# Backward pass of a convolution block with a gated product: one slab's pass over dh becomes a pass over two slabs with 512 columns

## The chip, the cores and the metric

The kernel runs on one core of a Trainium2 chip, in one launch. The metric is the device time in microseconds (us), the median of several runs. The engines of the core are named as the profile names them: PE multiplies matrices (PEld is its weight load, which runs beside it), DVE and ACT work on vectors, POOL and SP here mostly issue transfers. A transfer that is issued by SP, ACT or POOL stands in that engine's own queue, and an engine works its instructions off in order.

## The reference, cut to what matters

There are 2048 rows (S), 1024 columns (D) and 3584 hidden columns (F). The reference returns the output and the gradients of this function with respect to q, k, v, the taps, the filters and the three weight matrices:

```python
def _A_ref(q, k, v, shift_k, ssm_k, ssm_D):      # per column: 4 taps, then a long convolution
    k_shift = sum(k_pad[:, t:t + S, :] * shift_k[:, 3 - t] for t in range(4))
    kv = k_shift * v
    y = causal_conv(kv, ssm_k) + kv * ssm_D      # by FFT of length 2 S
    return q * y
def _B_ref(x, w_gate, w_up, w_down):
    g, u = x @ w_gate, x @ w_up
    h = g * u
    return h @ w_down
xn = _layernorm(A_q)
out = A_q + _A_ref(xn, k, v, ...) * silu(_B_ref(xn, w_gate, w_up, w_down))
```

The change concerns mostly the gradient of `_B_ref`. With dB the gradient of its result, dh = dB @ w_down.T, then dg = dh * u and du = dh * g, and the weight gradients are xn.T @ dg, xn.T @ du and h.T @ dB.

## The kernel before, in words

The work stands in one program whose parts overlap. In the order of PE's time:

1. Layer norm, and the gate and up products, in 14 slabs of 256 hidden columns (`gu_unit`, L655). u and g of a slab go to the buffer GUd in memory. The forward convolution runs on DVE beside it in `conv_forward` (L740); `shift` (L758) multiplies k by the taps, which lie spread over all partitions in `Wbc` (L128), four taps by 1024 columns. `spread` (L150) fills `Wbc` from memory, through POOL's queue.
2. The down product and the gate (`late_mm`, L1368, and `gate`, L1296). It leaves dB in memory (DBMd) and, turned, in four buffers DBMT (U10, U8, U4, U5), one for each 512 rows.
3. The stage of dh and of the two weight gradients, L1447 to L1552. It is the one that is changed most, and is described below.
4. The gradient of w_down (L1587), and then the gradient of the input with the layer norm's backward pass (`dx_part`, L1641, `ln_backward`, L1664). Beside that DVE works off the gradient of k and of the taps (`dk_units`, L1204), which reads `Wbc` again.

In stage 3 a half (`dh_half`, L1471) is dh of one slab for 1024 rows. It has two groups g of four row blocks. A matmul takes a 128 x 128 block of DBMT as its weights and the slab's turned rows of w_down, `wdt`, as the moving operand with 256 columns (L1482). Eight of them add up one row block, and two row blocks share one PSUM tile of 512 columns. ACT copies each tile into `dht` (L1484). When a group is complete, `multiply` (L1487) multiplies u and g of these four blocks by dht on DVE, in place (one instruction of 128 x 2048, recorded under the helper's line L212); after the second group the whole tile is stored to DGd through SP. u and g of a half come in through SP beforehand (`gu_in`, L1343): one of five buffers of 1 MB, two or three halves ahead.

`dw_slab` (L1495) has eight steps dc, one for each 128 columns of D. A step is 16 matmuls of 512 columns over all 2048 rows (L1499), with the first half's tile for rows 0 to 1023 and the second half's for the rest. ACT copies the sum into `wb` (three buffers, each for two steps), and SP stores it. After each step one group of the next slab's dh runs (`next(others)`), so that dh of slab s + 1 is spread over steps 0 to 3 of slab s. `load_wdt` (L1328) turns the 256 rows of w_down for slab s + 2 on the way in, through SP, in step 3 of slab s (two buffers, in the pool `bw`).

Beside it DVE works off the backward convolution: first eight forward transforms of dy (`dy_forward`, L1080), whose results go to memory (DYFd) through POOL, then 16 products and inverse transforms. `btick` (L1459) hands DVE so much of this work after each group on PE as keeps both in step. From the start of stage 3 DVE's instructions are kept in the order in which the program writes them; the same holds for POOL's transfers. ps_b has four PSUM tiles, in turn, for the groups of L1482 and L1499.

Of the kernel before, what the change touches and what calls it, by code (L numbers as in the profile page):

```python
# [19 lines left out]
def build_kernel(  # L20
# [107 lines left out]
    Wbc = const.tile([P, 4, D], BF16, name="Wbc")  # L128

    tip = tc.alloc_tile_pool(name="tip", bufs=1)  # L130
    TI = tip.tile([P, 2, 8, 2, P], BF16, name="TI")
# [9 lines left out]
    def load_bcast(bsb):  # L141

        wrow = bsb.tile([1, D, 4], BF16, name="wrow")
        st(wrow[:].rearrange("p d j -> p (d j)"), A_shift_k.rearrange("(o d) j -> o (d j)", o=1))
        wtap = bsb.tile([1, 4, D], BF16, name="wtap")

        def turn(j):
            nc.gpsimd.tensor_copy(wtap[:, j, :], wrow[:, :, j])

        def spread():  # L150
            st(WTd.rearrange("(o x) -> o x", o=1), wtap[:].rearrange("p j d -> p (j d)"))
            st(Wbc[:].rearrange("p j d -> p (j d)"), bass.AP(WTd.tensor, WTd.offset, [[0, P], [1, 4 * D]]))
        return turn, spread

    def angles(tg):
# [378 lines left out]
    Dz = kst.tile([P, D], BF16, name="Dz")  # L534
    V.memset(Dz[:], 0.0)
    krow = kst.tile([P, 2, 11, 256], BF16, name="k")
    V.memset(krow[0:1, 0, 0:3, :], 0.0)
    bsb = pool("bc_sb", 1)
    tg = pool("tg", 1)
# [200 lines left out]
    def conv_forward():  # L740
        S_ = conv_state

        def load_kv(dp, c):
            S_["k", dp] = krow
            if dp > 0 or c == 0:
                for i in range(2) if dp == 0 else (c,):
                    cld_k(krow[:, i], i, dp)
            if dp > 0 or c == 1:
                for i in range(2) if dp == 0 else (c,):
                    v = U[4][:, 2048 * i:2048 * i + 2048].rearrange("p (a x) -> p a x", a=8)  # L750
                    cld_v(v, i, dp * 256, 256)
# [6 lines left out]
        def shift(dp):  # L758
            kv = cx.tile([P, NB, 256], BF16, name="kv")
            S_["kvt", dp] = kv  # L760
            k = S_.pop(("k", dp))
            wb = lambda j: Wbc[:, j:j + 1, dp * 256:(dp + 1) * 256].unsqueeze(1).to_broadcast([P, 2, 8, 256])
# [12 lines left out]
            yield 2.3  # L775
# [294 lines left out]
    while conv_state["filters"]:  # L1070
        bm_first([fc_])
        fc_ += 1
    bw = pool("bw", 2, side="right")
    mh = [pool("mh0", 1, side="right")]
    ps_bx = pool("ps_bx", 1, space=PSUM)

# [106 lines left out]

    def dh_tail(ds, G, ew):
        hr = ew.tile([P, 2, 8, P], BF16, name="yl")
        ho = ew.tile([P, 2, P, 8], BF16, name="ho")
        for c in range(2):
            for rq in range(2):
                ps = ps_y4[0].tile([P, 4, P], F32, name="psY")
                for i in range(4):  # L1190
                    r = 4 * rq + i
                    for k in range(2):
                        nc.tensor.matmul(ps[:, i, :], G[:, 2 * r + k, c * P:(c + 1) * P], TI[:, 0, r, k, :],  # L1193
                                         start=(k == 0), stop=(k == 1))
# [9 lines left out]
    def dk_units(ew):  # L1204
# [9 lines left out]
        def load_turned(i):  # L1214
# [7 lines left out]
                nc.sync.dma_start_transpose(out=dkT[:], in_=DKSHd[ds, c * H:c * H + H, :])  # L1222
            return kT, dkT

        dk = load_rows(0)
        yield 3
        for i in range(16):
            ds, c = divmod(i, 2)
            dsl = slice(ds * P, (ds + 1) * P)
            wb = lambda j: Wbc[:, j:j + 1, dsl].to_broadcast([P, 8, P])  # L1230
# [95 lines left out]
            defer(turn)  # L1326

    def load_wdt(sl):  # L1328
        wdt = bw.tile([P, DC, SLW], BF16, name="wdt")
        wdt_ld[0] = nc.sync.dma_start_transpose(out=wdt[:], in_=B_w_down[sl * SLW:(sl + 1) * SLW, :])  # L1330
        return wdt

    def load_ht(bp):
        ht = mh[bp % 2].tile([P, NF, 256], BF16, name="ht")
# [1 line left out]
            last = ld(ht[:, f0:f1], ht_rows(bp, f0, f1))  # L1336
        return (lambda fc: ht[:, fc]), last

    DGU = {}
    wdts = []  # L1340
    wdt_ld = [None]

    def gu_in(k):  # L1343

        if k < 2 * NSL:
            t = U[(11, 6, 2, 3, 12)[k % 5]][:].rearrange("p (a b f) -> p a b f", b=8, a=2)
            ld(t, GUd[k // 2, k % 2])
            DGU[k] = t

    with tc.issue_after(ht1[1].ins):  # L1350
        ht2 = load_ht(2)
    bm_first(range(fc_, NF))
    room = [bw.tile([P, DC, SLW], BF16, name="wdt")[:].rearrange("p (i x) f -> p i (x f)", i=2) for i in range(2)]
# [61 lines left out]
    for bp in range(2, 8):  # L1415
# [6 lines left out]
        with tc.issue_after(row_ld[0].ins):  # L1422
            if bp in (4, 5, 7):
                q = (4, 5, 7).index(bp)
                dma_t = nc.sync.dma_start_transpose(out=DBMT[q], in_=DBMd[512 * q:512 * q + 512, :])
            if bp == 6:
                wdts.append(load_wdt(0))
                dma_t = wdt_ld[0]
        with tc.issue_after(dma_t.ins) if dma_t is not None else nullcontext():
            rows_in[2 * bp + 1] = gate_rows(2 * bp + 1)  # L1430
        if bp > 5:
            with tc.issue_after(row_ld[0].ins):
                gu_in(0) if bp == 6 else wdts.append(load_wdt(1))
        for i in range(2):
            n = (2 * bp + i - 2) * NF
            while done < n + NF:
# [11 lines left out]

    XN = [u8(q, a=4) for q in (7, 0, 1, 9)]
    bg = pool("bg", 2, side="right")  # L1450
    U.append(bg.tile([P, 4096], BF16, name="U12", bufs=1))
    ps_b = ps_tr = pool("ps_b", 4, space=PSUM)
    tr_name[0] = "psb"
    ps_c3 = pool("ps_c3", 2, space=PSUM)
# [6 lines left out]
        bpump((bcnt[0] - 10) / (BT - 10))  # L1461

    todo = []

    def after_group(n):
        flush(2)
# [1 line left out]
            todo.pop(0)()  # L1468
        btick(n)

    def dh_half(k, wdt):  # L1471

        sl, hf = divmod(k, 2)
        dgu = DGU[k]
        for g in range(2):
            dht = bg.tile([P, 4, SLW], BF16, name="dht", bufs=3)
            for e in range(2):
                ps = ps_b.tile([P, 512], F32, name="psb")
                for x in range(2):
                    b = 4 * g + 2 * e + x  # L1480
                    for dc in range(DC):
                        nc.tensor.matmul(ps[:, x * SLW:(x + 1) * SLW], DBMT[2 * hf + g][:, dc, (b % 4) * P:(b % 4 + 1) * P],  # L1482
                                         wdt[:, dc, :], start=(dc == 0), stop=(dc == DC - 1))
                nc.scalar.copy(out=dht[:, 2 * e:2 * e + 2].rearrange("p b f -> p (b f)"), in_=ps[:])  # L1484
                after_group(1)

            def multiply(g=g, dht=dht):  # L1487
                bs = slice(4 * g, 4 * g + 4)
                tt(dgu[:, :, bs], dgu[:, :, bs], dht[:].unsqueeze(1).to_broadcast([P, 2, 4, SLW]), MUL)
                if g == 1:  # L1490
                    ld(DGd[sl, :, 1024 * hf:1024 * hf + 1024, :].rearrange("a (u b) f -> u a b f", u=P), dgu)
            todo.append(multiply)
            yield

    def dw_slab(sl, dgus, others):  # L1495
        for dc in range(DC):
# [28 lines left out]
    for k in (3, 4):  # L1525
        gu_in(k)
    DBM = [u8(q, a=4) for q in (10, 8, 4, 5)]
    HSL = (3, 11, 6)
    hs = {}
    PIN[0] = PINQ[0] = True  # L1530
    for k in range(2):
        run(dh_half(k, wdts[0]))
    todo.pop()()
    for sl in range(NSL):
        if sl + 1 == NSL:
            load_h(0)
            for q in range(4):
                ld(DBM[q], DBMd[512 * q:512 * q + 512, :].rearrange("(b u) d -> u b d", u=P))
            load_h(1)

        def halves():
            for k in (2 * sl + 2, 2 * sl + 3):
                if k < 2 * NSL:
                    yield from dh_half(k, wdts[sl + 1])
        dw_slab(sl, [DGU[2 * sl], DGU[2 * sl + 1]], halves())
        for k in (2 * sl + 5, 2 * sl + 6):
            gu_in(k)
# [260 lines left out]
```

## Time and profile before

| what | before |
|---|---|
| median of 3 runs (lowest to highest) | 1911.96 us (1911.43 to 1912.38) |
| the profiled execution's own time | 1911.63 us |
| its span, first to last instruction | 1909.9 us |
| PE busy | 1899.4 us (99%), 11379 matmuls |
| PEld, DVE, ACT, POOL busy | 1013.9, 1549.7, 636.8, 332.7 us |
| PE busy from 0 to 700 us, 700 to 1317 us | 693.01 of 700, 616.88 of 617 us |
| PE busy from 1317 to 1506 us, 1506 to 1910 us | 189.00 of 189, 400.46 of 404 us |
| DVE busy in the same four stretches | 628.03, 546.51, 151.45, 223.70 us |
| granted clock of PE in all of them | 1.00 |
| share of the DMA engines in them | 0.79, 0.77, 0.83, 0.82 |
| chain that ended last | 97% PE |

Stage 3 runs from 700 to 1317 us. Matmuls are pipelined in the records: the "mean ns of one" of a group is how long one is on its way, and the pace is read from a run of them (a row of the chain or of the timeline says how many started in which time). A row of the timeline gives the start in us, the time in us, the engine, the line, the operation, output and inputs, the count, and in brackets the idle time before it and what ended it. SPq and POOLq are the instructions that issue transfers.

### The profile page before, as it was taken

The page shows a single profiled execution, that of the slowest core. Times are in us where ns is not written, and L with a number is a line of the kernel's source. Part 1 is how long each engine was busy: PE and PEld are TensorE (multiplying, and loading weights), DVE is VectorE, ACT ScalarE, POOL GpSimd, SP SyncE. Part 2 cuts the span into 40 slices and gives each one's busy share as a digit, 9 for nine tenths or more (in the row PEclk, how much of TensorE's full clock was granted, in tenths as well). Part 3 has the DMA queues.
Part 4 walks back from the last instruction along what each step waited for, and adds up shares of the span by engine and source line. Part 5 has one row for each costly group of instructions (what it writes and reads, how often), then busy time and mean ns, then how long its engine had stood idle before and what let it go on. Part 6 is the DMA issues. An engine that isn't in the chain of part 4 may idle for free.

```text
span 1909.9 us, 28150 instructions
## 1 busy us (share of the span) xinstructions
PE 1899.4 (99%) x11379; PEld 1013.9 (53%) x11379; DVE 1549.7 (81%) x1711; ACT 636.8 (33%) x927; POOL 332.7 (17%) x465
## 2 busy tenths in 40 slices
PE   8999999999999999999999999999999999999999
PEld 5555555545444466666666665664444444444444
DVE  8999999999988556887999999999995305788862
ACT  5765555556333233432222222222222102111121
POOL 5121211201113220001031221211212101111120
PEclk9999999999999999999999999999999999999999
DMA  9777766769769997677897798585887999989852
GB/s 298 269 263 233 251 208 223 252 211 311 241 227 307 316 314 231 209 231 233 264 277 247 231 266 258 184 286 180 230 238 181 219 206 190 194 187 190 194 166 88
DMA packets 425106, 444.34 MB, mean 233 GB/s; under 512 B 268400, under 2 KB 342796, under 8 KB 410512
## 3 DMA queue, kind: packets, MB, share of 16 engines
q1 hardware_dynamic: 367504, 239.03, 45.9%
q0 software_dynamic: 41152, 174.15, 29.0%
q10 hardware_dynamic: 16320, 29.36, 4.1%
q8 instruction: 89, 1.46, 0.3%
q14 instruction: 41, 0.34, 0.1%
HBM read 193.87 MB, written 189.84 MB: 201 GB/s over the span
## 4 chain that ended last, share of the span: by engine, by line
PE 97%; DVE 1%; ACT 1%; DMA 0%; issue 0%; SPq 0%; ACTq 0%
PE psb L1499 20%; PE psx L1644 20%; PE psg L671 19%; PE psb L1482 10%; PE psbm L1034 10%; PE psb L1582 9%; PE psF L234 3%; PE psI L455 1%; PE tr L565 1%; PE psY L1193 1%; PE psY L445 1%; PE psx L1582 1%; DVE bst L578 0%; DMA wslab<-in_B_w_gate_dram 0%; PE tr L788 0%; DVE U L212 0%
## 5 line engine op out<-in xcount | busy, mean ns | idle before, releaser
L671 PE MATMUL psg<-wslab,U 128*128 128x512 bf16 x1792 | 401.8, 379 | 3.5 <-DMA wslab<-in_B_w_gate_dram 2.1
L1499 PE MATMUL psb<-U,U 128*128 128x512 bf16 x1792 | 397.1, 379 | 0.0
L1644 PE MATMUL psx<-U,dgut 128*128 128x512 bf16 x1536 | 332.8, 379 | 0.0
L1644 PEld LDWEIGHTS <-dgut 128*128 128x128 bf16 x1792 | 175.3, 98 | 211.4
L1499 PEld LDWEIGHTS <-U 128*128 128x128 bf16 x1792 | 175.2, 98 | 198.0
L671 PEld LDWEIGHTS <-U 128*128 128x128 bf16 x1792 | 172.6, 98 | 197.2 <-issue 3.6
L1482 PE MATMUL psb<-wdt,U 128*128 128x256 bf16 x1792 | 205.6, 273 | 0.0
L1482 PEld LDWEIGHTS <-U 128*128 128x128 bf16 x1792 | 175.2, 98 | 29.2
L212 DVE TENSOR_TENSOR W<-W 128x1024 f32<-128x1024 f32 (+1 forms) x189 | 186.5, 1003 | 4.1
L1582 PE MATMUL psb<-U,U 128*128 128x512 bf16 x816 | 177.3, 379 | 0.0
L1504 ACT CAST wb<-psb 128x512 bf16<-128x512 f32 x112 | 65.6, 586 | 315.4 <-PE psb L1499 310.5
L1249 DVE SCALAR_TENSOR_TENSOR dkp<-dkT,kT 128x1024 bf16<-128x1024 bf16 (+2 forms) x64 | 78.3, 1223 | 93.1 <-DMA dkT<-DKSHd 91.4
L1034 PE MATMUL psbm<-U,ht 128*128 128x512 bf16 x672 | 146.0, 379 | 0.0
L1582 PEld LDWEIGHTS <-U 128*128 128x128 bf16 x896 | 87.4, 98 | 104.4
L673 ACT CAST gut<-psg 128x512 bf16<-128x512 f32 x156 | 91.5, 589 | 120.2 <-PE psg L671 119.7
L1676 ACT ACTIVATE dx_t<-dxn 128x1024 bf16<-128x1024 f32 x15 | 15.9, 1057 | 324.7 <-DVE dxn L212 324.7
L1034 PEld LDWEIGHTS <-ht 128*128 128x128 bf16 x672 | 65.7, 98 | 78.1
L212 DVE TENSOR_TENSOR U<-U,dht 128x2048 bf16<-128x2048 bf16 x56 | 68.3, 1220 | 46.5 <-ACT dht L1484 46.5
L1484 ACT CAST dht<-psb 128x512 bf16<-128x512 f32 x112 | 65.6, 587 | 116.4 <-PE psb L1482 116.4
L66 POOL DMA_DIRECT2D Hd<-hN x54 | 36.6, 677 | 268.9 <-DVE hN L212 258.9
L1623 ACT CAST wbs<-psb 128x512 bf16<-128x512 f32 x51 | 29.9, 586 | 145.4 <-PE psb L1582 134.3
L212 DVE TENSOR_TENSOR W<-SP 128x1024 f32<-128x1024 f32 x64 | 74.1, 1218 | 1.3 <-ACT SP L295 0.8
(263 smaller groups left out, 2342.9 us busy)
## 6 DMA issues: line engine op xcount, KB each, us to landing
U<-GUd SPq DMA_DIRECT2D x28, 1024.0 KB, 9.3
DGd<-U SPq DMA_DIRECT2D x28, 1024.0 KB, 5.8
GUd<-gut ACTq DMA_DIRECT2D x39, 512.0 KB, 5.2
out_dram<-wb SPq DMA_DIRECT2D x112, 128.0 KB, 4.8
U<-Hd SPq DMA_DIRECT2D x14, 1024.0 KB, 6.6
Hd<-hN POOLq DMA_DIRECT2D x54, 256.0 KB, 4.5
HTd<-hT SPq DMA_DIRECT2D x24, 512.0 KB, 3.7
ht<-HTd SPq DMA_DIRECT2D x18, 512.0 KB, 7.5
```

The costliest lines, as they stand in the source:

```text
L212: pinned(V.tensor_tensor(o, a, b, op))
L234: mm = nc.tensor.matmul(ps[:, k].rearrange("p (c d) -> p c d", c=2), T[:, r, k, :], xr[:, r], start=(n == 0), stop=(n == len(rs) - 1 and ( ...
L671: gu_mm[0] = nc.tensor.matmul(ps[:], XNT[q][:, dc, qi * P:(qi + 1) * P], w[:, dc].rearrange("p a f -> p (a f)"), start=(dc == 0), stop=(dc ...
L673: nc.scalar.copy(out=gut[:, :, i], in_=ps[:].rearrange("p (a f) -> p a f", a=2))
L1034: mm = nc.tensor.matmul(ps[:, dh * 512:(dh + 1) * 512], ht(fc)[:, i * P:(i + 1) * P], WD[fc // 4][:, fc % 4, dh * 512:(dh + 1) * 512], sta ...
L1249: ins = V.scalar_tensor_tensor(prod[:].rearrange("p r d -> p (r d)")[:, lo:H], dkT[:, 0, lo:H], 1.0, kT[:, 0, 13 + m + lo:13 + m + H], op0 ...
L1482: nc.tensor.matmul(ps[:, x * SLW:(x + 1) * SLW], DBMT[2 * hf + g][:, dc, (b % 4) * P:(b % 4 + 1) * P], wdt[:, dc, :], start=(dc == 0), sto ...
L1484: nc.scalar.copy(out=dht[:, 2 * e:2 * e + 2].rearrange("p b f -> p (b f)"), in_=ps[:])
L1499: nc.tensor.matmul(ps[:], XN[b // 4][:, b % 4, dc * P:(dc + 1) * P], dgus[b // 8][:, :, b % 8], start=(b == 0), stop=(b == NB - 1))
L1504: nc.scalar.copy(out=wb[:, dc % 2].rearrange("p a f -> p (a f)"), in_=ps[:])
L1582: nc.tensor.matmul(ps, h[:, f, b, :], DBM[b // 4][:, b % 4, dh * 512:(dh + 1) * 512], start=(b == 0), stop=(b == NB - 1))
L1644: nc.tensor.matmul(ps[:, dh * 512:(dh + 1) * 512], t[n][:, f, i * P:(i + 1) * P], WGU[n][:, f, dh * 512:(dh + 1) * 512], start=(n == 0 and ...
```

## The change

dh is now worked out for two slabs at a time. A matmul takes the same weights, and as its moving operand 2 x 256 columns, those of both slabs; eight of them fill a PSUM tile for one row block. Halves and groups are kept: `dh_pair(p, hf)` is dh of slabs 2p and 2p + 1 for 1024 rows. Half 0 of pair p + 1 runs in steps 4 to 7 of slab 2p, half 1 in steps 2 to 5 of slab 2p + 1 (two PSUM tiles behind each of these steps); pair 0 runs ahead of slab 0. `multiply` does one instruction for each slab of the pair, so two in a row. `dht` of the first group has one buffer of its own, that of the second uses half of the table TI, which nothing reads any more.

The turned rows lie in four buffers (WDT): two in `bw` and two in a new tile of `bg`. They are loaded a pair ahead, four before the stage and the others in step 5 of odd slabs and step 1 of even ones. u and g have six buffers instead of five (U13 is added) and are loaded in another order.

The room comes from the taps. `Wbc` (1024 columns for the whole kernel) is gone. `WB` holds two quarters of 256 columns; the first two are loaded in one transfer on SP's queue, the third and fourth on POOL's just ahead of the loads of k. `dk_units` loads its own quarters (`wbk`, two buffers), through POOL. `ho` of the last inverse transforms shares a buffer with `vl`.

```diff
-            st(Wbc[:].rearrange("p j d -> p (j d)"), bass.AP(WTd.tensor, WTd.offset, [[0, P], [1, 4 * D]]))
+            load_taps(WB[:].rearrange("p j e d -> p j (e d)"), 0, 512, ld)
...
+            if dp > 1 and c == 0:
+                load_taps(WB[:, :, dp % 2], dp * 256, 256)
...
+            if i % 4 == 0:
+                wbk = ew.tile([P, 4, 256], BF16, name="wbk", bufs=2)
+                load_taps(wbk[:], ds * P, 256)
...
-    def dh_half(k, wdt):
+    def dh_pair(p, hf):
+        if 2 * p >= NSL:
+            return
+        both = (2 * p, 2 * p + 1)
         for g in range(2):
-            dht = bg.tile([P, 4, SLW], BF16, name="dht", bufs=3)
-            for e in range(2):
+            dht = bg.tile([P, 4, 2, SLW], BF16, name="dht", bufs=1)[:] if g == 0 else dht_own
+            for x in range(4):
                 ps = ps_b.tile([P, 512], F32, name="psb")
-                for x in range(2):
-                    b = 4 * g + 2 * e + x
-                    for dc in range(DC):
-                        nc.tensor.matmul(ps[:, x * SLW:(x + 1) * SLW], DBMT[2 * hf + g][:, dc, (b % 4) * P:(b % 4 + 1) * P],
-                                         wdt[:, dc, :], start=(dc == 0), stop=(dc == DC - 1))
-                nc.scalar.copy(out=dht[:, 2 * e:2 * e + 2].rearrange("p b f -> p (b f)"), in_=ps[:])
+                for dc in range(DC):
+                    nc.tensor.matmul(ps[:].rearrange("p (j f) -> p j f", j=2), DBMT[2 * hf + g][:, dc, x * P:(x + 1) * P],
+                                     WDT[p % 2][:, :, dc, :], start=(dc == 0), stop=(dc == DC - 1))
+                nc.scalar.copy(out=dht[:, x].rearrange("p j f -> p (j f)"), in_=ps[:])
                 after_group(1)
+                if x == 1:
+                    yield
             def multiply(g=g, dht=dht):
                 bs = slice(4 * g, 4 * g + 4)
-                tt(dgu[:, :, bs], dgu[:, :, bs], dht[:].unsqueeze(1).to_broadcast([P, 2, 4, SLW]), MUL)
-                if g == 1:
-                    ld(DGd[sl, :, 1024 * hf:1024 * hf + 1024, :].rearrange("a (u b) f -> u a b f", u=P), dgu)
+                for j, sl in enumerate(both):
+                    dgu = DGU[sl, hf]
+                    tt(dgu[:, :, bs], dgu[:, :, bs], dht[:, :, j].unsqueeze(1).to_broadcast([P, 2, 4, SLW]), MUL)
+                    if g == 1:
+                        ld(DGd[sl, :, 1024 * hf:1024 * hf + 1024, :].rearrange("a (u b) f -> u a b f", u=P), dgu)
...
             after_group(2)
-            if dc == 3 and sl + 2 < NSL:
-                wdts.append(load_wdt(sl + 2))
-            next(others, None)
+            if 0 <= dc - (2 if sl % 2 else 4) < 4:
+                next(others, None)
+            n = sl + 5 if sl % 2 == 1 and dc == 5 else sl + 5 if sl % 2 == 0 and dc == 1 else NSL
+            if n < NSL:
+                load_wdt(n)
...
-    for k in (1, 2):
-        gu_in(k)
+    for k in ((1, 0), (0, 1), (1, 1)):
+        gu_in(*k)
+    for sl in (2, 3):
+        load_wdt(sl)
...
+        gu_room += [DGU_U[sl, 0], DGU_U[sl, 1]]
+        for k in ((sl + 2, 1), (sl + 3, 1)) if sl % 2 == 0 else ((sl + 3, 0), (sl + 4, 0)):
+            gu_in(*k)
```

More of the change, by code (lines that the diff above doesn't have):

```diff
@@ L536, in build_kernel, with load_taps @@
     krow = kst.tile([P, 2, 11, 256], BF16, name="k")
+    WB = kst.tile([P, 4, 2, 256], BF16, name="WB")
+    def load_taps(t, d0, w, queue=st):
+        queue(t, bass.AP(WTd.tensor, WTd.offset + d0, [[0, P], [D, 4], [1, w]]))
     V.memset(krow[0:1, 0, 0:3, :], 0.0)
@@ L1072, in build_kernel @@
         fc_ += 1
-    bw = pool("bw", 2, side="right")
+    bw = pool("bw", 1, side="right")
+    WDT = [bw.tile([P, 2, DC, SLW], BF16, name="wdt0")]
     mh = [pool("mh0", 1, side="right")]
@@ L1223, in load_turned @@
             return kT, dkT
+        wbk = None
         dk = load_rows(0)
@@ L1328, in load_wdt @@
     def load_wdt(sl):
-        wdt = bw.tile([P, DC, SLW], BF16, name="wdt")
-        wdt_ld[0] = nc.sync.dma_start_transpose(out=wdt[:], in_=B_w_down[sl * SLW:(sl + 1) * SLW, :])
-        return wdt
+        wdt_ld[0] = nc.sync.dma_start_transpose(out=WDT[sl // 2 % 2][:, sl % 2], in_=B_w_down[sl * SLW:(sl + 1) * SLW, :])
     def load_ht(bp):
@@ L1337, in load_ht, with gu_in @@
         return (lambda fc: ht[:, fc]), last
-    DGU = {}
-    wdts = []
+    DGU, DGU_U = {}, {}
     wdt_ld = [None]
[L1343 to L1348, printed above, removed]
+    gu_room = [11, 6, 12, 2, 13, 3]
+    def gu_in(sl, hf):
+        if sl < NSL:
+            DGU_U[sl, hf] = gu_room.pop(0)
+            DGU[sl, hf] = U[DGU_U[sl, hf]][:].rearrange("p (a b f) -> p a b f", b=8, a=2)
+            ld(DGU[sl, hf], GUd[sl, hf])
     with tc.issue_after(ht1[1].ins):
@@ L1352, in build_kernel @@
     bm_first(range(fc_, NF))
-    room = [bw.tile([P, DC, SLW], BF16, name="wdt")[:].rearrange("p (i x) f -> p i (x f)", i=2) for i in range(2)]
+    room = [WDT[0][:, n].rearrange("p (i x) f -> p i (x f)", i=2) for n in range(2)]
     bms = [out_of(pss[i], room[0][:, i]) for i in range(2)]
@@ L1426, in build_kernel @@
             if bp == 6:
-                wdts.append(load_wdt(0))
+                load_wdt(0)
                 dma_t = wdt_ld[0]
@@ L1450, in build_kernel @@
     bg = pool("bg", 2, side="right")
-    U.append(bg.tile([P, 4096], BF16, name="U12", bufs=1))
+    U += [bg.tile([P, 4096], BF16, name=f"U{i}", bufs=1) for i in (12, 13)]
+    WDT.append(bg.tile([P, 2, DC, SLW], BF16, name="wdt1", bufs=1))
     ps_b = ps_tr = pool("ps_b", 4, space=PSUM)
@@ L1463, in build_kernel @@
     todo = []
+    dht_own = TI[:, 1].rearrange("p r k f -> p (r k f)").rearrange("p (x j f) -> p x j f", x=4, j=2)
     def after_group(n):
@@ L1520, in build_kernel @@
         e[0] = -2
-    for k in (1, 2):
-        gu_in(k)
+    for k in ((1, 0), (0, 1), (1, 1)):
+        gu_in(*k)
+    for sl in (2, 3):
+        load_wdt(sl)
     for q in range(4):
         ld(XN[q], xnn[:, q // 2, 4 * (q % 2):4 * (q % 2) + 4, :])
-    for k in (3, 4):
-        gu_in(k)
+    for k in ((2, 0), (3, 0)):
+        gu_in(*k)
     DBM = [u8(q, a=4) for q in (10, 8, 4, 5)]
@@ L1530, in build_kernel @@
     PIN[0] = PINQ[0] = True
-    for k in range(2):
-        run(dh_half(k, wdts[0]))
+    for hf in range(2):
+        run(dh_pair(0, hf))
     todo.pop()()
+    load_wdt(4)
     for sl in range(NSL):
-        if sl + 1 == NSL:
+        if sl + 2 == NSL:
             load_h(0)
@@ L1538, in build_kernel @@
                 ld(DBM[q], DBMd[512 * q:512 * q + 512, :].rearrange("(b u) d -> u b d", u=P))
+        if sl + 1 == NSL:
             load_h(1)
[L1541 to L1547, printed above, removed]
+        dw_slab(sl, [DGU[sl, 0], DGU[sl, 1]], dh_pair(sl // 2 + 1, sl % 2))
+        gu_room += [DGU_U[sl, 0], DGU_U[sl, 1]]
+        for k in ((sl + 2, 1), (sl + 3, 1)) if sl % 2 == 0 else ((sl + 3, 0), (sl + 4, 0)):
+            gu_in(*k)
         if 0 < sl < 5:
```

11 lines of the change are left out of this document (4 added, 7 removed).

## The prediction

> **What bounds the kernel.** I read the page first, then the chain that ended last, then the timelines of DVE and SP between 845 and 950 us, and the DMA issues there.
>
> ```profile
> PE 1899.4 (99%) x11379; PEld 1013.9 (53%) x11379; DVE 1549.7 (81%) x1711; ACT 636.8 (33%) x927; POOL 332.7 (17%) x465
> ...
> L1499 PE MATMUL psb<-U,U 128*128 128x512 bf16 x1792 | 397.1, 379 | 0.0
> ...
> L1482 PE MATMUL psb<-wdt,U 128*128 128x256 bf16 x1792 | 205.6, 273 | 0.0
> ```
>
> PE is busy in 99% of the span, and neither line of the changed stage has idle time before it. So only PE time counts: fewer matmuls gain what they leave free on PE, and any wait that a matmul now meets is lost. The pace stands in two rows of the chain in order of time (start, us, what):
>
> ```profile
> 881.94 17.27 PE psb L1499 x80
> 899.21 3.49 PE psb L1482 x32
> ```
>
> 80 matmuls of 512 columns in 17.27 us are 215.9 ns each, 32 of 256 columns in 3.49 us are 109.1 ns. Two narrow ones cost 218.2 ns, one wide one 215.9.
>
> **What goes.** 1792 matmuls at L1482 become 896 with 512 columns. From start to start, over all neighbours of one line in the records, a narrow one takes 109.17 ns and a wide one 215.84 ns. The gain is 896 x (2 x 109.17 - 215.84) = 2.2 us. The moving operand is two runs of 256 columns; L1499 already reads two such runs at this pace. The 896 weight loads that go (98 ns each) lie beside matmuls and are worth nothing.
>
> A rule speaks of more. The Trainium skill (TensorE: Matmul & The Clock Gate, Back-to-back issue gap) says that in a stream of weight loads and matmuls both set the pace, about 131 ns at 512 columns and 81 ns at 128; with an estimated 98 ns for 256 between them, the 896 pairs would give 58 us. The rows disagree: 215.9 ns at 512 columns, and the next row gives (1.95 - 0.22) / 31 = 56 ns at 128, each with its own weight load.
>
> ```profile
> 1232.01 1.95 PE L1193 MATMUL psY<-TI,B 128*128 128x128 bf16 x32
> ```
>
> **What stays.** 112 copies on ACT, 56 multiplications on DVE (1.22 us each, now two in a row), the bytes through SP: the same. In the order in which the changed kernel is built, PE's instructions are the same up to 700 us and all engines do the same work behind 1317 us, but for the taps. So the question is whether PE meets a wait in stage 3. I laid PE's new order end to end from 700.05 us (0.2158, 0.1092 and 0.056 us for 512, 256 and 128 columns), and DVE's order at its rows' durations, each multiplication not before its last dht copy (0.8 us behind PE). Laid so, the old order gives back the four late multiplications between 912 and 935 us within 0.2 us.
>
> Pair 0 takes 128 x 0.2158 + 0.45 (a transpose) = 28.1 us, so slab 0 starts at 728.1 instead of 714.5. The second half's product is ready 0.5 us before its matmul, as before. Its u and g (U12) now lie behind the gate's buffers, on DVE until 707.4; with 9.7 us of landing they are there at 717, wanted at 722. Slabs 2, 6, 8, 10 and 12 find their products 3.5 to 7.4 us early (even slabs had 10.8 to 16.1 us, because dh ended in step 3; now it ends two steps before the slab that reads it). Odd slabs have over 30 us.
>
> **Slab 4 is the tight one.** It starts at 907.8 and its 13th matmul, at 910.4, reads the second group of half 1. In the new DVE order that multiplication stands behind the first backward product. In the old order that product waited:
>
> ```profile
> 896.00 1.28 DVE L283 SCALAR_TENSOR_TENSOR DX<-W 128x512 bf16<-128x512 f32 x2
> 907.56 4.56 DVE L212 TENSOR_TENSOR m<-TF,B 128x4096 bf16<-128x4096 bf16 x3 [10.28 <-issue]
> 912.04 1.22 DVE L212 TENSOR_TENSOR U<-U,dht 128x2048 bf16<-128x2048 bf16 x1
> ```
>
> The 10.28 us are the store of the last DX (its room is used again by m): issued at 897.57, landed after 9.9 us, while SP loaded u and g for the next slab. Laid end to end, DX ends at 896.7 in the new order as well. With the same landing the product starts at 907.0, the multiplication ends at 912.8, and PE loses 2.4 us. But SP's two loads for the next slab now come behind 905 us, and POOL's 1 MB sum into out_0 (L1550) comes behind the store instead of ahead. All eight such stores have a median landing of 5.3 us. With it the multiplication ends at 908.0, 2.4 us early. I take 5.3, because what delayed the one store has moved; bounds 0 and 2.4 us. What is late next is the first inverse matmul at 939, 2 to 6 us behind its data.
>
> **SP's queue.** Turns of w_down now come two in a row, behind the last dh matmul of a pair (900.9 us in slab 3), and behind them stand two loads of u and g, two stores DGd and the wb stores. One turn held SP for:
>
> ```profile
> L1330 SPq DMA_TRANSPOSE wdt<-in_B_w_down_dram x14: 1700/4910/12837, 644.9 to 1185.4; - x14
> ...
>   DMA out_dram<-wb: 2.9, 1
> ```
>
> (smallest, median, largest, ns; the second row, from the waits at L1504, shows that ACT waited once for a wb store already.) The wb buffer of steps 6 and 7 of slab 3 is wanted again by ACT at 925.3; PE then still has three PSUM tiles and stops at 932.0, so the store must land by 931.4. With medians: 900.9 + 2 x 4.9 + 1.5 of issues + 4.8 of landing = 917. With the worst rows (12.84 twice, landing 14.7, the median of wb stores between 880 and 910): 900.9 + 25.7 + 1.5 + 14.7 = 942.8, 11 us of stall. The nearest row is the 12.84 at 882, with POOL's loads under way as they will be here; the second turn meets them mostly done (4.9). With a landing halfway (9.8) that makes 930. I take 0, bounds 0 and 11 us. The Trainium skill (DMA: Bandwidth & Descriptors, Latency and other measured facts) gives 261 GB/s for turning transfers, an estimated 2.0 us for the 0.5 MB of a turn; by that this wait could not arise, but 12.84 us for issuing one alone says that it does not hold beside POOL's traffic.
>
> **The taps.** POOL loses one issue of 0.85 us ahead of the loads of k, for which DVE waited 1.32 us at 51 us; SP gains one that waits for WTd (issued at 27.5), with a landing of 4.5 us (POOL's 256 KB stores) done by 32. Behind it stand stores of hT and, at 63, the next weights: nobody is late. PE's gaps between 50 and 510 us add up to 1.8 us, so the taps give between 1.8 and, if SP's stores slip, -0.5 us; I take 0, since DVE falls back into PE's pace by 125 us. Quarters 3 and 4 are issued a slab ahead of their use. In `dk_units` four loads of 256 KB can each hold DVE by some 4.5 us; DVE is idle in 180 of the last 404 us, and PE has no wait for it there. Without that cover: 18 us of DVE, still no PE time.
>
> **Sum.** 1911.63 (the profiled execution's own time; span 1909.9) - 2.2 = 1909.4. The median of the runs is 0.33 above that execution, so 1909.8 for the median.
>
> **Rivals and chances.** A measurement of this kernel tells about 0.2% (3.8 us) from no change: below 1908.1 is faster, above 1915.8 slower.
>
> - A, the forecast: 2.2 us on PE and no new wait worth a microsecond: 1909.8 (1909 to 1911). 0.52.
> - B, slab 4 waits for DVE: up to 2.4 us, 1912.2. For it: the tight order; against: the store's path is freer. Decides where the store takes over 7.7 us. 0.15.
> - C, SP's double turns: the wb store lands late, ACT stops, four PSUM tiles fill, PE stands in slab 4. Up to 1909.8 + 11 = 1920.8; it ends above 1915.8 if the store lands after 937.4, that is if both turns and the landing take over 35 us (917 + 20.4). 0.18, of which 0.07 above 1915.8.
> - D, the taps' earlier start closes the early gaps as well: 1909.8 - 1.8 = 1908.0. Against: the gaps have other releasers too. 0.07, half of it below 1908.1.
> - E, the wide matmul over two tiles' rows does not run at L1499's pace (the moving rows now lie 4 KB apart): no gain, 1912.0. Against: L1499 reads rows as far apart. 0.06.
> - F, weight loads hold the array, so that 896 fewer give up to 896 x 98 ns = 88 us, 1824. Against: 56 ns between matmuls with a 98 ns load each. The skill's pace for such streams would be of this kind. 0.02.
>
> Faster 0.06 (half of D, F), slower 0.08 (C's tail and what I overlooked), same 0.86. The range is 1908.0 to 1914.2: it takes in A, B, D, E and the smaller part of C.
>
> **What would show it.** 896 matmuls of 512 columns at the dh line, 16 in 3.45 us; L1482's 205.6 us falls to about 200. Between 900 and 945 us: the idle time of PE at slab 4 (B: releaser DVE, the multiplication; C: ACT, wb), the wait of m<-TF,B, the time of the two turns. PE's gaps before 510 us show D. I am wrong if PE has more than a microsecond of new idle time in stage 3, or if anything behind 1317 us moves by more than the 2.2 us.

## The result, and the profile after

The changed kernel takes 1931.82 us (median of 5 runs, 1929.85 to 1935.64), against 1911.96 us (1911.43 to 1912.40): 1.0106 times as long, with a 95% interval of 1.0091 to 1.0120. The forecast was 1909.8, its range 1908.0 to 1914.2. The profiled execution has a span of 1930.1 us, 20.2 more than before.

The page of the changed kernel, the rows that answer to those of before (busy time, mean ns of one, then the idle time before them and what ended it):

```profile
PE 1901.5 (99%) x10483; PEld 926.5 (48%) x10483; DVE 1551.5 (80%) x1711; ACT 636.7 (33%) x927; POOL 335.6 (17%) x470
...
L1513 PE MATMUL psb<-U,U 128*128 128x512 bf16 x1792 | 397.2, 379 | 0.0
...
L1492 PE MATMUL psb<-wdt,U 128*128 128x512 bf16 x896 | 206.6, 385 | 16.5 <-ACT wb L1518 16.5
```

The 896 matmuls that the change left out are gone, and so are 87 us of weight loads. But the dh line, which had no idle time, now has 16.5 us, and ACT's copy into wb ends it. The timeline of PE says where. There are two stops. The first is in slab 4:

```profile
939.15 5.65 PE L1492 MATMUL psb<-wdt,U 128*128 128x512 bf16 x16 [5.63 <-ACT wb L1518]
944.64 3.62 PE L1513 MATMUL psb<-U,U 128*128 128x512 bf16 x16
```

The second, in the same timeline, is in slab 6:

```profile
1040.32 6.26 PE L1492 MATMUL psb<-wdt,U 128*128 128x512 bf16 x16 [10.84 <-ACT wb L1518]
1046.42 3.62 PE L1513 MATMUL psb<-U,U 128*128 128x512 bf16 x16
```

A second loss stands in the same rows: the 16 matmuls behind each stop take 5.65 and 6.26 us instead of 3.62. The windows give the granted clock (the third column from the right):

```profile
939.00:942.00 3.00, 2.85 (x7) 0.98 (x7) 2.11 (x2) 1.57 (x4) 0.00 (x0) 0.50 0.65 193
942.00:945.00 3.00, 3.00 (x12) 1.22 (x11) 0.00 (x0) 0.74 (x2) 0.00 (x0) 0.78 0.18 49
945.00:948.00 3.00, 3.00 (x16) 1.36 (x14) 2.54 (x3) 0.43 (x1) 0.00 (x0) 1.00 0.00 0
```

Behind the stop the clock is at half; in the records 10 matmuls behind the first stop and 13 behind the second start every 427 ns, and those that follow, at once, every 216. From start to start the two stops cost 5.8 + 11.0 us and the half clock 2.0 + 2.7 us.

The chain that ended last leads from the stop to its cause:

```profile
902.44 20.73 PE psb L1513 x96
...
923.20 0.59 ACT wb L1518
...
924.74 13.68 DMA out_dram<-wb
...
938.52 0.59 ACT wb L1518
...
939.15 5.65 PE psb L1492 x16
```

The store of steps 6 and 7 of slab 3, whose data ACT had ready at 910, was issued at 924.7 and landed 13.7 us later. SP's timeline shows what it stood behind:

```profile
902.47 19.53 SPq L1339 DMA_TRANSPOSE wdt<-in_B_w_down_dram  x2
922.10 0.53 SPq L61 DMA_DIRECT2D U<-GUd  x1
922.72 0.90 SPq L61 DMA_DIRECT2D DGd<-U  x2
923.71 1.58 SPq L61 DMA_DIRECT2D out_dram<-wb  x2
```

The first turn held SP for 13.90 us (its instruction lasted that long, and SP issued nothing else meanwhile), the second for 5.58; then come 3 MB of u, g and DGd, then wb:

```profile
L1339 SPq DMA_TRANSPOSE wdt<-in_B_w_down_dram x2: 5579/9740/13902, 902.5 to 916.4; - x2
```

In slab 6 the turns took 4.77 and 12.35 us, from 996.7 to 1013.9; 2 MB of DGd follow, and then the store of wb, whose second half was issued at 1023.2 and landed 16.4 us later. This is rival C of the prediction, twice.

The whole difference of the spans: - 2.2 (pace, measured below) + 16.8 (stops) + 4.7 (half clock) + 0.5 (a later start within the first 9 us) + 0.4 (behind the last matmul of stage 3) = 20.2 us.

### The profile page after: what moved, and what is told of

It is laid out like the page before. It is cut to its first block, busy times and chain, and to the rows that moved or that the text cites. A ratio compares the mean times of both kernels' runs of the same rounds, so it can differ in the third digit from the quotient of the medians.

```text
span 1930.1 us, 26354 instructions
## 1 busy us (share of the span) xinstructions
PE 1901.5 (99%) x10483; PEld 926.5 (48%) x10483; DVE 1551.5 (80%) x1711; ACT 636.7 (33%) x927; POOL 335.6 (17%) x470
## 4 chain that ended last, share of the span: by engine, by line
PE 94%; DVE 3%; DMA 2%; ACT 1%; SPq 0%; issue 0%; ACTq 0%
PE psx L1660 20%; PE psg L674 18%; PE psb L1513 18%; PE psbm L1039 10%; PE psb L1492 10%; PE psb L1598 9%; PE psF L233 3%; DMA out_dram<-wb 2%; PE psI L454 1%; PE tr L568 1%; PE psY L1199 1%; PE psx L1598 1%; PE psY L444 1%; DVE bst L581 0%; DVE U L211 0%; DMA wslab<-in_B_w_gate_dram 0%
## 5 line engine op out<-in xcount | busy, mean ns | idle before, releaser
L1513 PEld LDWEIGHTS <-U 128*128 128x128 bf16 x1792 | 175.2, 98 | 207.8
L674 PEld LDWEIGHTS <-U 128*128 128x128 bf16 x1792 | 172.6, 98 | 197.7 <-issue 3.3
L1492 PE MATMUL psb<-wdt,U 128*128 128x512 bf16 x896 | 206.6, 385 | 16.5 <-ACT wb L1518 16.5
L1492 PEld LDWEIGHTS <-U 128*128 128x128 bf16 x896 | 88.7, 99 | 123.0 <-issue 23.3
L1598 PEld LDWEIGHTS <-U 128*128 128x128 bf16 x896 | 87.4, 98 | 104.4
L233 PEld LDWEIGHTS <-TF 128*128 128x128 bf16 x560 | 53.9, 98 | 18.4 <-issue 3.1
L211 DVE TENSOR_TENSOR HX<-W 128x1024 bf16<-128x1024 f32 (+3 forms) x66 | 62.1, 990 | 0.1
## 6 DMA issues: line engine op xcount, KB each, us to landing
DGd<-U SPq DMA_DIRECT2D x28, 1024.0 KB, 10.6
```

Source lines behind the costliest of these rows:

```text
L211: pinned(V.tensor_tensor(o, a, b, op))
L233: mm = nc.tensor.matmul(ps[:, k].rearrange("p (c d) -> p c d", c=2), T[:, r, k, :], xr[:, r], start=(n == 0), stop=(n == len(rs) - 1 and ( ...
L674: gu_mm[0] = nc.tensor.matmul(ps[:], XNT[q][:, dc, qi * P:(qi + 1) * P], w[:, dc].rearrange("p a f -> p (a f)"), start=(dc == 0), stop=(dc ...
L1492: nc.tensor.matmul(ps[:].rearrange("p (j f) -> p j f", j=2), DBMT[2 * hf + g][:, dc, x * P:(x + 1) * P], WDT[p % 2][:, :, dc, :], start=(d ...
L1513: nc.tensor.matmul(ps[:], XN[b // 4][:, b % 4, dc * P:(dc + 1) * P], dgus[b // 8][:, :, b % 8], start=(b == 0), stop=(b == NB - 1))
L1598: nc.tensor.matmul(ps, h[:, f, b, :], DBM[b // 4][:, b % 4, dh * 512:(dh + 1) * 512], start=(b == 0), stop=(b == NB - 1))
```

## The experiments

Theory Q: the wb stores are late because they stand in SP's queue behind two turns in a row and the bulk behind these (the loads of u and g and the stores DGd). Its rivals: the DMA engines themselves are full (W), the rhythm of dh decides how late a store may be (R), POOL's transfers make the turns long (P). R and P can also hold together with Q. All edits are on the changed kernel unless said otherwise.

**Turns apart (e_apart).** The second turn of a pair goes behind the wb store of step 3 (`wst[0]` is the last wb store issued; `tc.issue_after` keeps what is issued inside it behind that store in SP's queue):

```
-            n = sl + 5 if sl % 2 == 1 and dc == 5 else sl + 5 if sl % 2 == 0 and dc == 1 else NSL
+            n = sl + 5 if sl % 2 == 1 and dc == 5 else sl + 5 if sl % 2 == 0 and dc == 3 else NSL
             if n < NSL:
-                load_wdt(n)
+                with tc.issue_after(wst[0].ins):
+                    load_wdt(n)
```

> The changed kernel, with the second turn of w_down of a pair held behind the wb store of step 3 of the even slab, so that the two turns no longer stand in a row on SP; everything else stays. In the changed kernel the two turns held SP for 13.9 + 5.6 us at 902 us and for 4.8 + 12.4 us at 997 us. If the double turn is the cause (theory Q in its first part): the store at slab 4 is issued 5.6 us and the one at slab 6 12.4 us earlier, which is as much as the stops (5.6 and 10.8 us), so both go but for a microsecond: 1910 to 1912 us. If what stands behind the turns (3 MB of u, g and DGd) or the full DMA engines sets the landing: at least the stop in slab 4 stays with 4 us or more, and the time is 1916 us or more.

Measured: 1910.26 us (1909.84 to 1912.89, 10 runs), 0.9992 of before (0.9982 to 1.0001). The dh line has no idle time left and the clock is 1.00 throughout. The row of the page:

```profile
L1492 PE MATMUL psb<-wdt,U 128*128 128x512 bf16 x896 | 201.9, 379 | 0.0
```

The first turn still took 14.2 us at 902. ACT still waited 8.7 us for a store, but PE's four PSUM tiles covered that. So moving the second turn alone takes the whole cost of the change away, and the time is within half a microsecond of what was forecast for the change (1909.8). The edit does two things at once, though: the turns are apart, and the second stands in another place; e_late below separates them.

**wb on ACT's queue (e_wbq).** `nc.scalar.dma_start(...)` in place of `ld(...)` for the 112 stores.

> The changed kernel, with the 112 stores of wb issued on ACT's queue instead of SP's; all else as it is. In the changed kernel PE stands idle twice for wb (5.6 us at 933 us, 10.8 us at 1029 us), and the 16 matmuls behind each stop take 2.2 and 2.8 us longer at a lower granted clock. Theory Q (the wb stores stand in SP's queue behind two turns of w_down and 3 MB of loads and stores): ACT's wait for wb and both stops go, PE is idle for under 1 us between 700 and 1330 us, and the time is 1931.8 - 16.5 - 5.0 = 1910.3 us (1909.5 to 1911.5). Rival W (the DMA engines themselves are full there, 400 GB/s and more between 920 and 940 us, whatever queue a store stands in): the stores land as late as before, ACT still waits over 10 us at each place, and the time stays above 1920 us. Rival D (DVE's second product at slab 4 becomes the bound as soon as wb is gone): 1910.3 plus up to 2.4 us, with PE waiting for DVE at its L1513 near 910 us.

Measured: 1917.08 us (1914.26 to 1924.12, 10 runs), 1.0027 (1.0018 to 1.0036); the profiled execution has 1912.5 us of span and 4.0 us of idle time at dh. That lies between the two expectations, and neither pure theory holds. Stores on a queue of their own, issued at 995.8, landed after 16.9 and 19.7 us; two stores issued at 985.5 took 3.4 and 4.4. Meanwhile the second turn held SP for 21.7 us, from 990.5. The windows of that stretch (last columns: clock, DMA share, GB/s):

```profile
989.00:996.00 7.00, 7.00 (x34) 3.20 (x33) 6.96 (x8) 1.17 (x2) 4.14 (x5) 1.00 1.19 245
996.00:1010.00 14.00, 14.00 (x67) 6.35 (x65) 13.72 (x15) 1.17 (x2) 0.56 (x1) 1.00 1.06 165
1010.00:1018.00 8.00, 5.92 (x36) 3.32 (x35) 4.58 (x4) 0.00 (x0) 0.00 (x0) 1.00 1.19 162
```

The DMA engines are fully taken at 165 GB/s, where they move 245 just before. So here a turn beside POOL's loads also delayed stores on another queue.

The stop of 2.9 us that is left has one more reason, which ACT's timeline shows:

```profile
1002.12 0.58 ACT L1518 CAST wb<-psb 128x512 bf16<-128x512 f32 x1 [2.87 <-PE psb L1513]
1012.12 5.92 ACTq L1522 DMA_DIRECT2D out_dram<-wb  x2
1018.16 1.07 ACT L1518 CAST wb<-psb 128x512 bf16<-128x512 f32 x2 [15.46 <-DMA out_dram<-wb]
```

The two stores whose data was ready at 1002.7 were issued at 1012.12 and 1017.67, and in the trace ACT's queue waits at both for a turn to land (1012.05 and 1017.64). ACT's next copy into wb stands behind them. So the store did not get free of the turns on ACT's queue, and this run does not separate the queue from the DMA engines cleanly: the idle time at dh fell from 16.5 to 4.0 us, and the rest is no measure of W.

**wb ahead of the bulk (e_first).** The turns stay in a row; the two DGd stores and the loads of u and g are issued behind the wb store of steps 6 and 7:

```
-                        ld(DGd[sl, ...], dgu)
+                        behind.append((DGd[sl, ...], dgu))
...
             after_group(2)
+            while dc % 2 == 1 and behind:
+                with tc.issue_after(wst[0].ins):
+                    ld(*behind.pop(0))
...
-            gu_in(*k)
+            with tc.issue_after(wst[0].ins):
+                gu_in(*k)
```

> The changed kernel, with the two turns in a row as they are, but with the two stores DGd and the loads of u and g of the next slabs issued behind the wb store of steps 6 and 7 of a slab instead of ahead of it. If the 3 MB ahead of the store in SP's queue are what makes it late: the store is issued right behind the turns (922 and 1014 us) and lands in some 5 us, before PE has to stop (933 and 1029 us): both stops go, 1910 to 1912 us. If the two turns alone are enough: the store still lands at 936 and 1034 us or later, both stops stay with more than half of their length, and the time is above 1920 us.

Measured: 1915.51 us (1911.46 to 1922.06, 10 runs), 1.0016 (1.0005 to 1.0028), between the two expectations. In the profiled execution (span 1909.8) the turns still took 13.66 + 5.47 us, and one stop of 1.35 us is left:

```profile
1036.55 3.61 PE L1492 MATMUL psb<-wdt,U 128*128 128x512 bf16 x16 [1.35 <-ACT wb L1518]
```

In slab 4 the store that the bulk had stood in front of now landed 2.1 us after its issue (922.08 to 924.15), where it took 13.7. So there the bulk made the landing late, and not full DMA engines in general (W). The stop that is left is not at this store: it comes from the stores of the next two steps, which now stand behind the bulk (issued at 1017.6 and 1018.0, landed after 14.9 and 17.8 us). The profiled execution is the second fastest (1911.60); in the six from 1915.46 us up, of which there is no trace, the mean granted clock is 0.997 to 0.999, so PE probably stopped in them, at places that are not known. Taking the bulk away from in front of the store gains 16.3 us of the 21.6 that taking the second turn away gains.

**dh two steps earlier (e_even).** In even slabs dh runs behind steps 2 to 5 instead of 4 to 7: `if 0 <= dc - 2 < 4` for all slabs.

> The changed kernel, with the four half groups of dh in an even slab run behind its steps 2 to 5 instead of 4 to 7; SP's work is the same. In the changed kernel seven steps of weight gradients (from step 6 of an odd slab to step 4 of the next) follow one another without dh, so that wb buffers are wanted every 6.9 us, where with dh between the steps it is every 13.8. Theory R (this rhythm sets how late a store may land): the step that waits comes two half groups (2 x 3.45 = 6.9 us) later, the stop in slab 4 (5.6 us) goes and that in slab 6 falls from 10.8 to about 4 us: 1930.1 - 16.5 - 5.0 + 4 + 2 = 1914.6 us of span, 1916 us. Rival (only how long SP is held counts, or the stop moves on to the next store): two stops of together over 12 us stay, above 1924 us.

Measured: 1912.54 us (1910.21 to 1923.84, 10 runs), 1.0010 (0.9997 to 1.0023), better than expected. The stop in slab 4 went although its turns took 13.62 + 5.46 us as before and the store landed at 937.5, as late as in the changed kernel (938.4): ACT waited 7.4 us for it, PE not at all. So the rhythm counts. The stop in slab 6 is no evidence for it: there the turns, at 988, happened to miss POOL's loads, and took 1.88 + 2.08. Another wait came in its place, of the kind of rival B:

```profile
1000.11 9.62 PE L1513 MATMUL psb<-U,U 128*128 128x512 bf16 x36 [2.23 <-DVE U L211]
```

The product of slab 6 is late for PE by 2.2 us; the half clock behind it costs 1.7 us more.

**POOL's sums later (e_sumlate).** `if 8 < sl < 13` instead of `if 0 < sl < 5` for the sums into out_0.

> The changed kernel, with POOL's four sums of 1 MB into out_0 moved from slabs 1 to 4 to slabs 9 to 12; the two turns stay in a row. Theory P (a turn holds SP until the data that POOL's queue has in flight has gone through: 13.9 us at 902 us beside 3.7 MB, about 2 us with nothing beside it): without the sum the first turn at 902 us holds SP for 3.7 us less or better (under 10.5 us), the stop in slab 4 falls from 5.6 to under 2.5 us, the one in slab 6 (no sum beside its turns) stays between 8 and 13 us, and the time is about 1924 us. Rival (the sum does not matter to the turn): 13 to 14 us of hold and both stops stay, 1931 us.

Measured: 1917.12 us (1914.05 to 1920.16, 8 runs), 1.0027 (1.0017 to 1.0037). The turns at 902 us (smallest, median, largest, ns; the smaller is the second turn):

```profile
L1339 SPq DMA_TRANSPOSE wdt<-in_B_w_down_dram x2: 2508/6975/11442, 902.2 to 913.7; - x2
```

13.95 us of hold instead of 19.5; the first turn is at 11.4 where under 10.5 was expected, the second gained 3.1 us, the first 2.5. The stop in slab 4 is gone, the one in slab 6 is left with 7.90 us. The direction is P's, and no more: the turns in slab 6, with no sum beside them, still took 6.54 + 10.32 us. The time is better than expected, because the whole stop in slab 4 went, its half clock with it, and the one in slab 6 shrank by 2.9 us.

**Both turns later, in a row (e_late).** From slab 2 on both are issued behind the wb store of step 3 of the even slab, by these lines in place of the two that load for `n`:

```
+            for n in (sl + 4, sl + 5) if sl % 2 == 0 and dc == 3 else ():
+                if 4 < n < NSL:
+                    with tc.issue_after(wst[0].ins):
+                        load_wdt(n)
```

> The changed kernel, with both turns of a pair in a row again, but issued behind the wb store of step 3 of the even slab (from slab 2 on) instead of behind the last dh matmul of the odd slab. This separates what e_apart changed together: that the turns are apart, and where they stand. Theory P and R together (a turn is slow only while other queues' data are in flight, and the stretch without dh is where a late store hurts): there the loads that POOL issues at 899 to 905 us have gone through, the next one (1 MB) comes at about 928, and the steps that follow alternate with dh; the two turns hold SP for under 13 us together (19.5 and 17.1 in the changed kernel), PE does not wait for wb, and the time is 1910.3 us (1909.8 to 1911.5). Rival (two in a row are too long wherever they stand): 17 us of hold or more, a stop of 3 us or more in slab 4 or 6, and 1915 us or more.

Measured: 1911.03 us (1909.82 to 1916.56, 10 runs), 0.9999 (0.9990 to 1.0009), and no wait for wb in stage 3. At 926 the two turns took 4.7 + 4.2 us and at 1011 2.9 + 2.2. At 1099 they met POOL's loads after all and held SP for 23.3 us, longer than any pair of the changed kernel:

```profile
1098.78 23.25 SPq L1339 DMA_TRANSPOSE wdt<-in_B_w_down_dram  x2
```

The timeline of PE beside it:

```profile
1100.48 3.62 PE L1492 MATMUL psb<-wdt,U 128*128 128x512 bf16 x16
1103.93 3.62 PE L1513 MATMUL psb<-U,U 128*128 128x512 bf16 x16
1107.39 3.62 PE L1492 MATMUL psb<-wdt,U 128*128 128x512 bf16 x16
1110.84 3.62 PE L1513 MATMUL psb<-U,U 128*128 128x512 bf16 x16
```

PE did not stop: here dh stands between the steps, and a wb buffer is wanted every 13.8 us. That agrees with R: 19.5 us of hold cost 7.8 us where seven steps follow one another, 23.3 us cost nothing here. A second thing differs: the store stands directly behind the turns, without the bulk, and landed at 1127.1. But ACT wanted its buffer again only at 1137.0, and PE had four tiles on top of that, so that a landing of 13.7 us (1138.0, an estimate) would have cost nothing either. The expected under 13 us of hold came true at 926 and 1011 and not at 1099, so the place does not keep the turns short; here it made a long one harmless. (The profiled execution is the longest of the ten: behind stage 3 a turn of w_gate held SP for 8.5 us, ACT waited 9.4 us for a store, and PE 3.6 us for ACT, the same kind of stop in another stage.)

**Two wb buffers (e_wb2).** `bufs=2`, one execution.

> The changed kernel with two wb buffers instead of three. Theory R (PE stops when the store of the buffer it needs has not landed, and in the stretches without dh a buffer fewer moves that point 6.9 us ahead): the stops in slabs 4 and 6 grow by 6.9 us each, to about 12.5 and 17.7 us, and stops appear at other turns where the slack was below 6.9 us; at least 1946 us. Besides it shows what a stop costs behind it: so far 2.9 us of idle time cost nothing, 5.6 us cost 2.2 us more and 10.8 us 2.8 us more over the next 16 matmuls, at a lower granted clock. Expected: nothing behind stops under 3 us, 2 to 3 us behind each of the long ones, not growing with their length.

Measured: 1941.26 us, below the expected 1946; two stops of 10.56 and 14.16 us at dh, no third. They began only some 3.6 us earlier and not 6.9: what PE has ahead is four PSUM tiles, and with dh between them four tiles are 10.4 us of work, without it up to 13.8, so that one buffer fewer does not simply add its two steps. Direction right, size half.

**The pace (e_apart_narrow).** e_apart, with each dh matmul of 512 columns made as two of 256 (`WDT[p % 2][:, j, dc, :]`, j = 0, 1).

> As e_apart (the two turns kept apart, 1910.26 us, PE idle for no wb), but each dh matmul of 512 columns is made as two of 256, as in the kernel before; order, turns and transfers stay. The forecast's first term (896 matmuls of 512 columns save 896 x 2.5 ns of PE's pace): stage 3 is 2.2 us longer than e_apart's and the time 1912.5 us. Rival E (no gain in pace): 1910.3 us. Rival F (weight loads cost time on PE): well above 1913 us.

Measured: 1912.57 us (1911.80 to 1913.91, 11 runs), 1.0002 (0.9993 to 1.0011); no idle time at dh either. Stage 3 lasts from 699.84 to 1316.82 = 616.98 us, in e_apart from 700.62 to 1315.36 = 614.74. The difference is 2.24 us: the first term of the forecast, and rivals E and F fall.

**The taps alone (e_taps).** The kernel before with only the change of the taps.

> The kernel before, with the change of the taps alone (quarters of 256 columns, the first two through SP's queue, the later ones and those of the gradient of k through POOL's); dh stays as it was. Forecast: 0, so 1912.0 us (1911.5 to 1912.5). Rival D (the earlier start closes PE's early gaps): 1910.2 us. If the slower early start of the changed kernel (its PE was 0.5 us later from 9 us on) comes from the taps: 1912.5 us, with the gap at the first loads of w_gate.

Measured: 1913.43 us (1912.25 to 1917.49, 11 runs), 1.0009 (1.0000 to 1.0018). That is not the gain of D, and above the forecast range. The profiled execution starts stage 3 at 700.36 us (before 700.05) and has one new wait of 0.95 us for dxn in the last stage. Whether the taps cost nothing, 0.5 or 1.5 us lies within the interval and stays open; e_apart_narrow, with the same change of the taps, starts stage 3 at 699.84, earlier than before.

**A try for better (e_apart_sumlate).**

> e_apart with POOL's four sums moved to slabs 9 to 12 as well: a try for a better version. PE waits for nothing in stage 3 of e_apart, so that there is nothing more to gain in the median: 1910.3 us (1909.8 to 1910.8), against 1912.0 of the kernel before. If the runs of e_apart above 1912 us (2 of 10) come from stores that land late beside the sums, none of these runs is above 1911.5 us. If the sums collide with something in slabs 9 to 12: above 1911 us in the median.

Measured: 1910.45 us (1909.61 to 1915.92, 10 runs), 0.9996 (0.9986 to 1.0005), the same as e_apart. One run at 1915.9 says that the sums were not what made single runs long. No version is clear of the kernel before: the intervals of the two fastest, e_apart and this one, both take in 1. PE is busy in 98 to 99% of every span, and the pace gives 2.2 us, no more.

## Why the prediction was wrong, step by step

- **The pace** was right: 2.2 us forecast, 2.24 measured. Weight loads that go are worth nothing, as said.
- **Stage 3's start and DVE** were right. Slab 0 starts at 728.6 (728.1 forecast). The tight product of slab 4 stood behind the store of DX as described, and that store landed as the median said:

```profile
903.93 4.56 DVE L211 TENSOR_TENSOR m<-TF,B 128x4096 bf16<-128x4096 bf16 x3 [5.90 <-DMA DYFd<-DX]
908.41 2.35 DVE L211 TENSOR_TENSOR U<-U,TI 128x2048 bf16<-128x2048 bf16 x2
```

  The first of these two multiplications is slab 4's; the second ended at 910.8, and PE did not wait; before, m had started at 907.56. B did not happen here, though e_even shows it in slab 6 as soon as dh moves.
- **SP's queue is the step that failed.** The mechanism, its place and its order of events were written down, then priced at 0 of 0 to 11 us. The estimate was a landing at 930; it was 938.4, 8.4 us later. Term by term: the turns began at 902.5 instead of 900.9 (1.6), took 13.90 + 5.58 instead of 12.84 + 4.9 (1.7), four issues stood ahead of the store, 2.7 us instead of 1.5 (1.2), and the landing took 13.7 instead of 9.8 (3.9). The last term is the largest. A middling value was taken for the landing, between the general median (4.8) and the 14.7 of the rows near it; of those six wb stores, issued between 895 and 908 us behind a single turn, four took 14.6 to 18.6 us and two 6.4 and 6.9. That 3 MB now stand directly ahead of the store in the same queue had no term of its own, and e_first shows what it is worth: 2.1 us of landing without them. The margin was 1.4 us, far less than the spread of these rows. PE's order was 1.4 us behind the laid one by then (slab 4 began at 909.2, not 907.8), which moved the deadline too: 8.4 - 1.4 - 1.4 = 5.6 us, the stop.
- **It was priced in one slab.** Slab 6 has the same order, and its stop is twice as long (10.8 us). That the second turn meets POOL's loads mostly done held in slab 4 (5.58 us), and not in slab 6 (12.35 us, with another load of 1 MB issued by POOL during the hold) or in e_wbq (21.7 us).
- **What a stop costs behind it** was left out: 4.7 us of half clock on top of 16.8 of stops. The 11 us given as the upper end could not have held the time.
- **The rhythm** was in the order that was laid, but not in the reasoning: seven steps of the weight gradients now follow one another where there were five (the row of 80 matmuls in the prediction), and want a wb buffer every 6.9 us. e_even shows in slab 4 that this decides whether a given hold of SP costs anything, and e_late agrees.
- **The taps**: D is wrong, PE is busy for 459.20 us between 50 and 510 us in both kernels. The cover named for the end of the kernel held: PE has no wait there.
- Of the rules weighed, the 261 GB/s for a turning transfer (the Trainium skill, DMA: Bandwidth & Descriptors, Latency and other measured facts) does not hold here: beside POOL's loads a turn of 0.5 MB landed 19.9 us after its issue.

## What to carry to other kernels

A transfer that can hold its queue for long is priced at every place where it is issued, with its own worst row, together with all that then stands ahead of the next store that somebody waits for; where the margin is smaller than the spread of the rows, the likeliest value is not zero. Putting work into bigger groups also bunches its loads and the work between: ask how fast each buffer is wanted in the stretches that become uniform. When a queue is late, moving one transfer (e_apart) can be worth more than giving the store another queue (e_wbq), where it may have to wait for the same transfers.

## What the runs showed of the hardware that was not expected

A turn of 0.5 MB holds SP for 1.3 to 2.9 us in the rows of all runs where POOL's queue moved nothing and SP's own at most 0.6 MB meanwhile. Beside other transfers it holds SP longer: 13.9 us beside 3.7 MB that POOL's queue moved within the hold, by its records, 11.4 beside 3.3 MB, 12.8 beside 3.4 MB in the kernel before. The bytes of POOL's queue alone do not set it: it was 12.35 us beside 1.0 MB (slab 6 of the changed kernel) and 17.3 beside 1.7 MB (e_late). What does stays open. And stores on another queue slow down as well (e_wbq).

After a stop PE ran at half its pace (427 ns for 512 columns, then 216) for 7 to 14 matmuls: 1.4 to 2.9 us behind stops of 2.2, 3.6, 5.6, 7.9, 10.6, 10.8 and 14.2 us, not growing with their length; none behind stops of 1.4 and 2.9 us. The records of the granted clock in the traces show why. Between the first and the last microseconds of the program the clock was half for 3.413, 6.827 or 13.653 us at a time, which is one, two or four steps of 3.413 us, and the full clock between two such stretches lasted whole steps as well (88.747 us in the changed kernel, 26 of them). Below stand three such steps of e_even, with its stop of 2.23 us from 997.88 on within the first, and then three of e_wbq, with its stop of 2.88 us from 1015.92 on across the border of the first two (the number behind the comma is PE's busy time, the third column from the right the clock):

```profile
997.14:1000.55 3.41, 1.18 (x7) 0.43 (x6) 3.38 (x4) 0.00 (x0) 1.63 (x3) 1.00 0.97 260
1000.55:1003.96 3.41, 3.41 (x10) 1.21 (x9) 3.38 (x6) 0.59 (x1) 2.72 (x4) 0.50 1.00 382
1003.96:1007.37 3.41, 3.41 (x17) 1.56 (x16) 3.34 (x3) 0.59 (x1) 0.56 (x1) 1.00 1.03 388
```

```profile
1013.92:1017.33 3.41, 2.00 (x11) 0.88 (x9) 0.72 (x1) 0.00 (x0) 0.00 (x0) 1.00 1.23 153
1017.33:1020.74 3.41, 1.94 (x10) 0.88 (x9) 0.00 (x0) 1.07 (x2) 0.00 (x0) 1.00 1.03 420
1020.74:1024.15 3.41, 3.40 (x16) 1.47 (x15) 0.00 (x0) 0.10 (x1) 0.00 (x0) 1.00 1.06 427
```

2.2 us idle within one step made the next step half; 1.4 and 1.5 us in two steps did not. So where a stop falls on these steps counts, and not its length alone. The Trainium skill (TensorE: Matmul & The Clock Gate, What's actually happening) describes a free-running window of 3.4 us and half clock after an idle one. The half pace and the steps of 3.41 us agree; e_even shows in addition that a window of which 1.18 us were busy was enough.
